# A conditioned transformer block on one core: second MLP product token-major, two head groups' denominators from the exps, prologue reordered, two scheduler constants changed

## The chip, the cores and the metric

The kernel runs on 1 core of one Trainium2 chip. The metric is the time on the device in microseconds (us), from the core's first instruction to its last and a little more; the profile's span is 1 to 3 us shorter than the time. The lower the better.

## The reference

One block: layer norm with conditioning, multi-query attention (32 heads of 32, one shared K and V), and a gated MLP. S = 2048 tokens, D = 1024, F = 3584, everything in bf16.

```python
mod = (silu(c) @ w_mod).reshape(1, 6, 1, -1)
sa, ca, ga, sb, cb, gb = ...                     # six rows of 1024
h = layernorm(x) * (1 + ca) + sa
q = h @ wq      # 32 heads of 32
k = h @ wk      # one head of 32, shared
v = h @ wv      # one head of 32, shared
p = softmax(q k^T * 32**-0.5)
x = x + ga * ((p v) @ wo)
h = layernorm(x) * (1 + cb) + sb
x = x + gb * ((silu(h @ w1) * (h @ w3)) @ w2)
```

## The kernel before

The kernel treats the tokens in 4 blocks of 512 queries. For each block there is `attention` (8 head groups of 4 heads) and then `post` (output projection, layer norm, first products with w1 and w3, second product with w2). The `post` of one block is interleaved with the `attention` of the next. What runs when is decided by a list scheduler inside the kernel: every operation is a node with an assumed duration; the scheduler walks through an imagined time and gives each engine, again and again, the best node that could start now. The result is a fixed instruction order per engine. Semaphores keep it correct; the assumed times set only the order and the PSUM banks (PSUM is where TensorE writes its results; the kernel uses it as 8 banks of 512 columns).

```python
def act_t(n):                         # assumed ScalarE time for n columns
    return n / 1200.0 + 0.115
...
# in schedule(): the pick on TensorE ("pe"); S = scores, V = value matmuls, D = denominators
    def key(c):
        s, n = c
        if n.cls == "S":
            r = 0
        elif n.cls is not None:
            r = 1 if att or t - n.est > 1.0 else 4
        else:
            r = 3                     # MLP and projection matmuls: the fill
        return (r, n.prio, n.seq)
pick = min((c for c in cands if c[0] <= t + (slack if c[1].prio <= 1 else 0.001)), key=key)
...
st = max(dma_free, s + 1.2)           # assumed DMA time
dma_free = st + n.nbytes / 230e3
```

Attention, per head group: 16 steps. A step makes scores for one tile of 128 keys and four heads (4 matmuls into PSUM), two exps of 128 x 1024 on ScalarE into one of `NU = 10` buffers, and after 8 steps a batch of 32 value matmuls that reads those 8 buffers. The softmax denominators come from VectorE, which adds four exp tiles into a partial sum (`TR`, 3 adds each), and 16 matmuls with ones over the four partial sums.

```python
NU = 10; VB = 8; NTR = 5
for s in range(ns):                   # 16 steps
    u = i % NU
    ...                               # scores -> SP, two exps SP -> U[u]
    if len(pend) == vb:               # every 8 steps: 32 value matmuls
        ...
    # partial sums on VectorE
    if w == 1:   TR[tr] = U[first_u] + U[u]
    elif w > 1:  TR[tr] = TR[tr] + U[u]
# denominators: ones x TR, 4 partial sums x 4 heads
```

Second product, with the output transposed (128 rows of D by 512 tokens), so it has to be turned back by transposes:

```python
for dt in range(NC):
    o2t[dt] = sum over fc of  W2S[fc].T @ HHT[fc, 0:512]     # 28 matmuls of 512 columns
    O2B = o2t[dt] * gate_column                              # VectorE
    transpose 4 x (128x128), then X += ...                   # TensorE, VectorE
```

Start: the loads stand in one queue in program order.

```python
xload(0, 4); <8 loads of modulation columns>; <wk, wv, wq part 0>; xload(4, 4); <wq rest>; <wo>
# then, with the work on the tiles: xload(8, 4), xload(12, 4)
```

The softmax here doesn't subtract the row's maximum and nothing guards it: scores larger than these inputs give would overflow.

Of the kernel before, what the change touches and what calls it, by code (L numbers as in the profile page):

```python
# [8 lines left out]
P = 128  # L9
# [4 lines left out]
class Node:  # L14
    __slots__ = ("eng", "fn", "dur", "lat", "deps", "prio", "seq", "mode", "acq", "touch",
                 "start", "vis", "pos", "ndeps", "users", "need_inc", "cnt", "dsem", "dval", "nbytes", "est", "cls",
                 "sbanks")
# [8 lines left out]
class Dag:  # L26
# [12 lines left out]
    def add(self, eng, fn, reads=(), writes=(), dur=0.1, lat=0.1, prio=5, mode=None, cls=None,  # L39
            acq=None, groups=(), seq=None, dkey=None, nbytes=0, sbanks=()):  # L40
# [41 lines left out]
        for d in n.deps:  # L82
            d.users.append(n)
        n.dsem = n.dval = None
# [9 lines left out]
    def schedule(self, banks):  # L94
# [8 lines left out]
        for n in self.nodes:  # L103
            n.ndeps = len(n.deps)
            n.est = 0.0
            if n.ndeps == 0:
                ready[n.eng].append(n)
# [28 lines left out]
        while left:  # L136
# [85 lines left out]
            if n.dsem is not None:  # L222
                st = max(dma_free, s + 1.2)
                dma_free = st + n.nbytes / 230e3
                n.vis = dma_free + 0.8
            else:
                n.vis = s + d + n.lat
            for u in n.users:
                u.ndeps -= 1
                if not (e == "pe" and u.eng == "pe"):  # L230
                    u.est = max(u.est, n.vis + SEM_LAT)
                if u.ndeps == 0:
                    ready[u.eng].append(u)
# [73 lines left out]
def act_t(n):  # L307
    return n / 1200.0 + 0.115
# [9 lines left out]
def build(nc, x_in, wq_in, wk_in, wv_in, wo_in, w1_in, w3_in, w2_in, c_in, wmod_in, out, S, D, F):  # L318
# [12 lines left out]
    R = 4  # L331
    NTR = 5
# [12 lines left out]
    WREG = sb("WREG", [P, 4 * 2048 + 2 * NF * P], BF16)  # L345
# [14 lines left out]
    NM = sb("NM", [P, NT], F32)  # L360
# [7 lines left out]
    O2B = HREG[:, o + 1024:o + 2048].rearrange("p (a s) -> p a s", a=2)  # L368
# [6 lines left out]
    U = UREG[:, 0:NU * 2048].rearrange("p (u g s) -> p u g s", u=NU, g=4)  # L375
    TR = UREG[:, NU * 2048:].rearrange("p (u g s) -> p u g s", u=NTR, g=4)
    WM01 = UREG[:, 0:NC * 2048].rearrange("p (c s) -> p c s", c=NC)
    assert (NU + NTR) * 2048 >= NC * 2048
    W1S = WREG[:, 0:2 * 2048].rearrange("p (a c f) -> p a c f", a=2, c=NC)
    W3S = WREG[:, 2 * 2048:4 * 2048].rearrange("p (a c f) -> p a c f", a=2, c=NC)  # L380
    W2S = WREG[:, 4 * 2048:].rearrange("p (a c f) -> p a c f", a=2, c=NF)
    WQ = WREG[:, 4 * 2048 - 2048:4 * 2048 - 2048 + NC * D].rearrange("p (c f) -> p c f", c=NC)
    WMS = WREG[:, 0:6144].rearrange("p (a c f) -> p a c f", a=3, c=4)
    GAB = WREG[:, 4 * 2048 - 2048 + NC * D:4 * 2048 - 2048 + NC * D + 1024]

    SP = nc.alloc_psum_tensor("SP", [P, 3, 2, 512], F32)
    PB = [nc.alloc_psum_tensor("PB%d" % i, [P, 512], F32)[:] for i in range(2)]
    PB += [SP[:, b, h, :] for b in range(3) for h in range(2)]
# [13 lines left out]
    def dma(fn, key, reads=(), writes=(), nbytes=0, prio=5, seq=None):  # L402
        return G.add("sp", fn, reads=reads, writes=writes, dur=0.06, dkey=key, nbytes=nbytes, prio=prio, seq=seq)
# [3 lines left out]
    def xload(t0, n):  # L407
        for t in range(t0, t0 + n):
            dma(lambda e, t=t: e.dma_start(X[:, t % NXS, :], x2[t * P:(t + 1) * P, :]),
                ("x", t % NXS), writes=[("X", t % NXS)], nbytes=P * D * 2)  # L410

    xload(0, 4)
    for k in range(NC):
# [7 lines left out]
    xload(4, 4)  # L421
    dma(lambda e: e.dma_start(WQ[:, :, P:D], wq_in[:, P:D].rearrange("(c p) f -> p c f", p=P)), "wq1",
        writes=[("WQ", 1)], nbytes=7 * P * D * 2)
    dma(lambda e: e.dma_start(WO[:], wo_in.rearrange("(c p) f -> p c f", p=P)), "wo", writes=["WO"], nbytes=D * D * 2)
# [41 lines left out]
    def ln_scale(t0, n):  # L466
        ks = [("MV", t0 + i) for i in range(n)]
        rk = [("RS", t0 + i) for i in range(n)]
        G.add("pool", lambda e: e.tensor_scalar(RS[:, t0:t0 + n], MV[:, t0:t0 + n, 1], EPS, None, ALU.add),
              reads=ks, writes=rk, dur=0.3)  # L470
        G.add("pool", lambda e: e.tensor_tensor(RS[:, t0:t0 + n], RS[:, t0:t0 + n], NHALF[:, 0:n], ALU.pow),
              reads=rk + ["NHALF"], writes=rk, dur=0.4)
        G.add("pool", lambda e: e.tensor_tensor(NM[:, t0:t0 + n], RS[:, t0:t0 + n], MV[:, t0:t0 + n, 0], ALU.mult),
              reads=rk + ks, writes=[("NM", t0 + i) for i in range(n)], dur=0.3)

    def ln_norm(t, q):
        s = t % NXS
        G.add("dve", lambda e: e.tensor_scalar(XN[:, q, :], X[:, s, :], RS[:, t:t + 1], NM[:, t:t + 1],
                                               ALU.mult, ALU.subtract),
              reads=[("X", s), ("RS", t), ("NM", t)], writes=[("XN", q)], dur=0.5, prio=2)  # L480

    def ln_transpose(nt, q0, dst, dkeys, fs, fm, engs, prio=5):
# [3 lines left out]
        for cb in range(NC // ncb):  # L486
            g = grp()
            for i in range(nt):
                def tr(e, i=i, g=g, cb=cb):
                    for h in range(ncb):  # L490
                        c = cb * ncb + h
                        r = e.transpose(PBH[g.bank][:, h * w + i * P:h * w + (i + 1) * P],
                                        XN[:, q0 + i, c * P:(c + 1) * P], IDENT[:])
                    return r
                G.add("pe", tr, reads=[("XN", q0 + i), "IDENT"], dur=ncb * 0.065, lat=0.2,
                      acq=g if i == 0 else None, groups=[(g, "w")], mode="F", prio=prio)
            for h in range(ncb):
                c = cb * ncb + h
                en = engs[cb % len(engs)]
                if en == "act":  # L500
# [4 lines left out]
                        dur=act_t(w) + 0.19, prio=2)  # L505
# [49 lines left out]
    for tb in range(NTB):  # L555
        for i in range(4):
            ln_stats(tb * 4 + i)
        ln_scale(tb * 4, 4)
        for i in range(4):
            ln_norm(tb * 4 + i, i)  # L560
        if tb + 2 < NTB:
            xload(tb * 4 + 8, 4)
        ln_transpose(4, 0, lambda c, tb=tb: HT[:, c, tb * 512:(tb + 1) * 512],
                     lambda c, tb=tb: [("HT", c, tb)], 0, 1, ("act", "dve") if tb == 0 else ("dve",))
        kv(tb)
        if tb == 0:
            qproj(0, 0)
    for f in range(1, NC):
# [5 lines left out]
    nwm = 0  # L574
    GAK = [("GAB",)]
    for h in range(2):
        g = grp()
        for kb in range(2):
            sl = nwm % 3
            nwm += 1  # L580
            dma(lambda e, kb=kb, h=h, sl=sl: e.dma_start(
                WMS[:, sl], wmod_in[kb * 512:(kb + 1) * 512, 2 * D + h * 512:2 * D + (h + 1) * 512]
                .rearrange("(c p) f -> p c f", p=P)), ("wms", sl), writes=wms(sl), nbytes=P * 2048 * 2)
            def mm(e, kb=kb, sl=sl, g=g):
                for k in range(4):
                    i = e.matmul(PB[g.bank], SCB[kb * 4 + k], WMS[:, sl, k, :],
                                 start=(kb == 0 and k == 0), stop=(kb == 1 and k == 3))
                return i
            G.add("pe", mm, reads=SCBK + wms(sl), dur=4 * MM, lat=0.2, acq=g if kb == 0 else None,
                  groups=[(g, "w")], mode="F")  # L590
        G.add("dve", lambda e, g=g, h=h: e.tensor_copy(GAB[:, h * 512:(h + 1) * 512], PB[g.bank]),
              writes=[("GAB", h)], groups=[(g, "r")], dur=dve_t(512), prio=4)
    for f in range(NC):
        G.add("dve", lambda e, f=f: e.tensor_tensor(WO[:, f, :], WO[:, f, :], GAB, ALU.mult),
              reads=["WO", ("GAB", 0), ("GAB", 1)], writes=[("WOG", f)], dur=dve_t(1024, 2), prio=6)
    for m in range(3):
        g = grp()
        for h in range(2):
            for kb in range(2):
                sl = nwm % 3  # L600
                nwm += 1
# [14 lines left out]
        a, b2 = ((1.0, 0.0), (1.0, 1.0), (0.5, 0.0))[m]  # L616
        G.add("dve", lambda e, g=g, m=m, a=a, b2=b2: e.tensor_scalar(
            MODC[:, 3 + m, :], PB[g.bank][:, 0:8], a, b2, ALU.mult, ALU.add),
            writes=[("MODC", 3 + m)], groups=[(g, "r")], dur=0.15, prio=4)
    for tb in range(1, NTB):  # L620
# [7 lines left out]
    def attention(q0, qn):  # L628
        npk = 512 // qn
        ns = NT // npk  # L630
        per_t = ns // (R // npk)
        vb = VB // npk
        for f in range(NC):
            pend = []
            trs = []
            for s in range(ns):
# [3 lines left out]
                bufs = [(2 * i) % 3, (2 * i + 1) % 3]  # L640
                kts = [s * npk + j for j in range(npk)]

                def smm(e, f=f, kts=kts, bufs=bufs):
                    for j, kt in enumerate(kts):
                        for gg in range(4):
                            r = e.matmul(SP[:, bufs[gg // 2], gg % 2, j * qn:(j + 1) * qn],  # L646
                                         KT[32 * gg:32 * gg + 32, kt * P:(kt + 1) * P],
                                         QT[32 * gg:32 * gg + 32, f, q0:q0 + qn], start=True, stop=True,
                                         tile_position=(32 * gg, 0))
                    return r  # L650
                G.add("pe", smm, reads=sorted({("KT", kt // 4) for kt in kts}) + qkeys(f, q0, qn),
                      writes=[("SP", b) for b in bufs], dur=npk * qn / 2400 + 0.027 * npk, lat=0.2, prio=0, cls="S",
                      mode="S", sbanks=[2 + 2 * b + h for b in bufs for h in range(2)])
                uk = [("UR", u)]
                for h in range(2):
                    G.add("act", lambda e, u=u, h=h, b=bufs[h]: e.activation(  # L656
                        U[:, u, 2 * h:2 * h + 2, 0:npk * qn], SP[:, b, :, 0:npk * qn], ACT.Exp, scale=SCALE),
                        reads=[("SP", bufs[h])], writes=[("U", u, h)] + (uk if h == 0 else []), dur=act_t(2 * npk * qn),
                        prio=0, sbanks=[2 + 2 * bufs[h] + a for a in range(2)])
                ur = [("U", u, 0), ("U", u, 1)] + uk  # L660
                pend.append((u, kts))
                if len(pend) == vb:
                    g = grp()
                    last = len(pend) - 1
                    for w0 in range(0, len(pend), 2):
                        def pv(e, part=tuple(pend[w0:w0 + 2]), f=f, g=g, w0=w0, last=last):
# [231 lines left out]
```

## Time and profile before

| before | |
|---|---|
| time, median of the first 3 runs (lowest to highest) | 1310.71 us (1310.08 to 1313.36) |
| span, mean granted clock of TensorE | 1308.6 us, 0.935 |
| first exp, exp no. 25, exp no. 257, end of last exp | 29.2, 83.7, 320.6, 1107.7 us |
| exps | 1024, started 0.905 us apart (median of all start-to-start times) |

The first view is the page: busy time of each engine, then the busy tenths in 40 slices of 32.7 us. "PEclk" is the granted clock in tenths.

```profile
span 1308.6 us, 21172 instructions
...
PE 1138.8 (87%) x8561; PEld 439.4 (34%) x8689; DVE 958.9 (73%) x1206; ACT 1015.3 (78%) x1142; POOL 17.1 (1%) x35
...
PE   5387896455779999999899999999999999999998
...
ACT  1368988999999999999979999998999998011100
PEclk8688996666889999999999999999999999999999
```

ScalarE is full up to slice 34 and then almost empty; TensorE is full from about slice 12 to the end. So there is an attention stretch, in which exps and matmuls both nearly fill their engine, and a tail that is matmuls alone. I cut the span at exp no. 25 (the first that needs late K tiles), at exp no. 257 (the first of block 1) and at the end of the last exp. The windows view of before gives, for each stretch, its length and then busy time and instruction count by engine:

```profile
core 0: us, PE busy (x) PEld busy (x) DVE busy (x) ACT busy (x) POOL busy (x), PEclk, DMA share, GB/s
0.00:83.70 83.70, 42.40 (x506) 24.94 (x511) 58.05 (x116) 26.80 (x30) 8.87 (x23) 0.76 0.58 197
83.70:320.60 236.90, 166.88 (x1467) 54.83 (x1480) 168.47 (x186) 216.42 (x232) 0.00 (x0) 0.78 0.17 46
320.60:1107.70 787.10, 735.70 (x5611) 269.45 (x5703) 655.67 (x782) 755.37 (x853) 6.77 (x9) 0.99 0.32 84
1107.70:1308.60 200.90, 193.85 (x980) 90.15 (x997) 76.71 (x122) 16.74 (x29) 1.47 (x3) 0.99 0.53 127
```

Blocks 1 to 3 (third row) have ScalarE busy for 755 of 787 us and TensorE for 736. The tail (fourth row) has TensorE busy for 194 of 201.

Where ScalarE idles at the start: its timeline (start, length, engine, line, operation, count, and in brackets the idle time before it and what ended it), and below it two lines of the DMA queue.

```profile
39.96 9.27 ACT L656 ACTIVATE UREG<-SP 128x1024 bf16<-128x1024 f32 x10 [0.82 <-PE SP L646]
73.86 7.44 ACT L656 ACTIVATE UREG<-SP 128x1024 bf16<-128x1024 f32 x8 [24.64 <-PE SP L646]
83.73 20.84 ACT L656 ACTIVATE UREG<-SP 128x1024 bf16<-128x1024 f32 x22 [2.43 <-PE SP L646]
```

```profile
21.33 10.25 SPq L581 DMA_DIRECT2D WREG<-in_w_mod_dram  x3
31.70 39.35 SPq L409 DMA_DIRECT2D X<-in_A_x_dram  x16
```

The x tiles stand behind the modulation and weight loads, and exp no. 17 waits 24.64 us for scores whose K comes from those tiles.

```profile
437.35 6.94 ACT L656 ACTIVATE UREG<-SP 128x1024 bf16<-128x1024 f32 x7
```

Seven fill matmuls stand in one interval between scores, the 32 value matmuls in the next, 2.2 us each. The exp pair that covers an interval takes 1.8 us; ScalarE shows no wait here.

### The profile page before, as it was taken

The page shows a single profiled execution, that of the slowest core. Times are in us where ns is not written, and L with a number is a line of the kernel's source. Part 1 is how long each engine was busy: PE and PEld are TensorE (multiplying, and loading weights), DVE is VectorE, ACT ScalarE, POOL GpSimd, SP SyncE. Part 2 cuts the span into 40 slices and gives each one's busy share as a digit, 9 for nine tenths or more (in the row PEclk, how much of TensorE's full clock was granted, in tenths as well). Part 3 has the DMA queues.
Part 4 walks back from the last instruction along what each step waited for, and adds up shares of the span by engine and source line. Part 5 has one row for each costly group of instructions (what it writes and reads, how often), then busy time and mean ns, then how long its engine had stood idle before and what let it go on. Part 6 is the DMA issues. An engine that isn't in the chain of part 4 may idle for free.

```text
span 1308.6 us, 21172 instructions
## 1 busy us (share of the span) xinstructions
PE 1138.8 (87%) x8561; PEld 439.4 (34%) x8689; DVE 958.9 (73%) x1206; ACT 1015.3 (78%) x1142; POOL 17.1 (1%) x35
## 2 busy tenths in 40 slices
PE   5387896455779999999899999999999999999998
PEld 3133331111223333333333333333333333444443
DVE  5768786666798888778978887789888887643421
ACT  1368988999999999999979999998999998011100
POOL 1000000000000000000000000000000000000000
PEclk8688996666889999999999999999999999999999
DMA  9415104000003333342423333441533334375545
GB/s 313 151 41 178 33 1 110 12 1 1 1 1 97 98 97 97 94 85 57 120 78 94 95 94 94 93 77 29 157 97 98 97 97 85 77 175 147 160 83 118
DMA packets 253504, 118.93 MB, mean 91 GB/s; under 512 B 121312, under 2 KB 245216, under 8 KB 253408
## 3 DMA queue, kind: packets, MB, share of 16 engines
q1 hardware_dynamic: 253408, 117.59, 33.9%
q8 instruction: 68, 1.11, 0.4%
q14 instruction: 28, 0.23, 0.1%
HBM read 113.38 MB, written 4.19 MB: 90 GB/s over the span
## 4 chain that ended last, share of the span: by engine, by line
PE 58%; ACT 25%; DVE 9%; issue 6%; DMA 1%; POOL 1%; SPq 0%; DVEq 0%; ACTq 0%
ACT UREG L656 24%; PE PB L765 13%; PE PB L794 10%; PE PB L670 8%; PE SP L646 7%; PE SP L765 6%; PE SP L794 4%; PE PB L546 3%; PE PB L738 2%; ACT HREG L774 2%; DVE UREG L697 2%; DVE ST L461 1%; DVE UREG L702 1%; PE PB L712 1%; PE SP L738 1%
## 5 line engine op out<-in xcount | busy, mean ns | idle before, releaser
L656 ACT ACTIVATE UREG<-SP 128x1024 bf16<-128x1024 f32 x1024 | 968.5, 1067 | 85.5 <-PE SP L646 65.9
L765 PE MATMUL PB<-QT,WREG 128*128 128x512 bf16 x1397 | 343.3, 381 | 9.1 <-issue 6.4
L702 DVE TENSOR_TENSOR UREG<-UREG 128x2048 bf16<-128x2048 bf16 x256 | 310.5, 1213 | 38.4 <-ACT UREG L656 35.9
L646 PE MATMUL SP<-QT,KT 32*128 32x512 bf16 x2048 | 215.4, 411 | 100.0 <-ACT UREG L656 93.9
L697 DVE TENSOR_TENSOR UREG<-UREG 128x2048 bf16<-128x2048 bf16 x128 | 155.8, 1217 | 70.0 <-ACT UREG L656 69.9
L765 PEld LDWEIGHTS PB<-QT,WREG 128*128 128x128 bf16 x1456 | 125.7, 98 | 176.2 <-issue 52.3
L646 PEld LDWEIGHTS SP<-QT,KT 32*128 32x128 bf16 x2048 | 52.0, 92 | 313.4 <-ACT UREG L656 287.0
L794 PE MATMUL PB<-HREG,WREG 128*128 128x512 bf16 x612 | 153.3, 380 | 4.0 <-issue 2.5
L670 PE MATMUL PB<-UREG,V 128*32 128x512 bf16 x2016 | 142.9, 419 | 6.2 <-ACT UREG L656 5.8
L721 DVE RECIPROCAL DSB<-DSB 128x128 f32<-128x128 f32 x128 | 115.5, 928 | 0.1
L774 ACT ACTIVATE HREG<-SP 128x512 bf16<-128x512 f32 x28 | 16.7, 597 | 126.8 <-PE SP L765 123.9
L781 DVE TENSOR_TENSOR HREG<-HREG,PB 128x512 bf16<-128x512 bf16 x98 | 66.3, 676 | 19.6 <-PE PB L765 18.6
L794 PEld LDWEIGHTS PB<-HREG,WREG 128*128 128x128 bf16 x644 | 55.3, 98 | 73.5 <-issue 22.9
L765 PE MATMUL SP<-QT,WREG 128*128 128x512 bf16 x330 | 74.5, 379 | 0.3
L670 PEld LDWEIGHTS PB<-UREG,V 128*32 128x32 bf16 x2016 | 48.0, 101 | 78.9 <-issue 32.4
L776 DVE SCALAR_TENSOR_TENSOR HREG<-HREG,PB 128x512 bf16<-128x512 bf16 x84 | 57.5, 685 | 13.0 <-ACT HREG L774 9.9
L546 PE MATMUL PB<-HREG,WREG 128*128 128x512 bf16 x243 | 62.2, 389 | 1.7 <-DVE QT L549 0.8
L774 ACT ACTIVATE HREG<-PB 128x512 bf16<-128x512 f32 x84 | 56.5, 672 | 6.9 <-PE PB L765 6.8
L794 PE MATMUL SP<-HREG,WREG 128*128 128x512 bf16 x245 | 56.0, 379 | 0.4
L738 PE MATMUL PB<-WO,QT 128*128 128x512 bf16 x193 | 51.0, 389 | 2.9 <-DVE X L741 1.2
L776 DVE SCALAR_TENSOR_TENSOR HREG<-HREG,SP 128x512 bf16<-128x512 bf16 x28 | 19.3, 688 | 43.4 <-ACT HREG L774 43.4
L765 PEld LDWEIGHTS SP<-QT,WREG 128*128 128x128 bf16 x336 | 32.8, 98 | 39.4
(81 smaller groups left out, 547.9 us busy)
## 6 DMA issues: line engine op xcount, KB each, us to landing
WREG<-in_B_w_dram SPq DMA_DIRECT2D x112, 512.0 KB, 3.9
WREG<-in_B_w_dram SPq DMA_DIRECT2D x32, 896.0 KB, 5.9
X<-in_A_x_dram SPq DMA_DIRECT2D x32, 256.0 KB, 3.6
WREG<-in_w_mod_dram SPq DMA_DIRECT2D x16, 512.0 KB, 5.0
UREG<-in_w_mod_dram SPq DMA_DIRECT2D x8, 512.0 KB, 7.9
out_dram<-X SPq DMA_DIRECT2D x16, 256.0 KB, 2.6
WO<-in_A_wo_dram SPq DMA_DIRECT2D x1, 2048.0 KB, 14.6
WREG<-in_A_wq_dram SPq DMA_DIRECT2D x1, 1792.0 KB, 9.6
```

What stands on the lines that cost most here:

```text
L546: g = mm_group(NC, lambda e, b, c: e.matmul(b, WQ[:, c, f * P:(f + 1) * P], HT[:, c, sl], start=c == 0, stop=c == NC - 1), lambda c: [("WQ ...
L646: r = e.matmul(SP[:, bufs[gg // 2], gg % 2, j * qn:(j + 1) * qn], KT[32 * gg:32 * gg + 32, kt * P:(kt + 1) * P], QT[32 * gg:32 * gg + 32, ...
L656: G.add("act", lambda e, u=u, h=h, b=bufs[h]: e.activation(U[:, u, 2 * h:2 * h + 2, 0:npk * qn], SP[:, b, :, 0:npk * qn], ACT.Exp, scale=S ...
L670: r = e.matmul(PB[g.bank][32 * gg:32 * gg + 32, 0:qn], V[:, kt, :], U[:, pu, gg, j * qn:(j + 1) * qn], start=w0 + n == 0 and j == 0, stop= ...
L697: G.add("dve", lambda e, tr=tr, u=u, fu=first_u: e.tensor_tensor(TR[:, tr, :, 0:npk * qn], U[:, fu, :, 0:npk * qn], U[:, u, :, 0:npk * qn] ...
L702: G.add("dve", lambda e, tr=tr, u=u: e.tensor_tensor(TR[:, tr, :, 0:npk * qn], TR[:, tr, :, 0:npk * qn], U[:, u, :, 0:npk * qn], ALU.add), ...
L721: G.add("dve", lambda e, h=h: e.reciprocal(DSB[:, h * 128:(h + 1) * 128], DSB[:, h * 128:(h + 1) * 128]), reads=["DSB"], writes=[("DSBr", ...
L738: g = mm_group(NC, lambda e, b, f, t=t, h=h: e.matmul(b, QT[:, f, t * P:(t + 1) * P], WO[:, f, h * 512:(h + 1) * 512], start=f == 0, stop= ...
L765: return e.matmul(b[:, o:o + qn], w13[w][:, sl, c, sub * P:(sub + 1) * P], QT[:, c, q0:q0 + qn], start=c == 0, stop=c == NC - 1)
L774: G.add("act", lambda e, g=g1: e.activation(TS[:, 0:qn], PB[g.bank][:, 0:qn], ACT.Tanh, scale=0.5), writes=["TS"] + alias("TS"), groups=[( ...
L776: G.add("dve", lambda e, g=g1: e.scalar_tensor_tensor(TT[:, 0:qn], TS[:, 0:qn], 1.0, PB[g.bank][:, 0:qn], ALU.add, ALU.mult), reads=["TS"] ...
L794: return e.matmul(b[:, j * qn:(j + 1) * qn], W2S[:, (d0 + j) % 2, fc, :], HHT[:, fc, 0:qn], start=fc == 0, stop=fc == NF - 1)
```

## The change

The change has several parts in one diff (cut to the core):

- **Second product token-major**: the activations are the stationary operand, `w2` streams, the output is token by D and needs no transposes. Matmuls are twice as many at half the columns. The gate becomes a row that is multiplied in at evacuation. The w2 slots share their space with those of w1 and w3, so each load is 1.75 MB.
- **Direct denominators** for two of eight head groups in blocks 1 to 3 (`NDIR = 2`): 32 more ones matmuls per batch of 8 steps instead of VectorE's adds.
- **LN2 per tile**, and the reciprocals of the last head group with higher priority.
- **Prologue**: 8 x tiles come first, then the modulation columns; the rest of wq, and wo, after all x loads. With it, x tiles 4 to 7 are normalised into other space, and half of the second tiles' evictions from PSUM go to ScalarE.
- **Two constants** of the scheduler: assumed ScalarE time (`act_t`, called the exp constant below) and assumed DMA rate.

```diff
 def act_t(n):
-    return n / 1200.0 + 0.115
+    return n / 1200.0 + 0.057
@@ schedule
-                dma_free = st + n.nbytes / 230e3
+                dma_free = st + n.nbytes / 300e3
@@ prologue
-    xload(0, 4)
+    xload(0, 8)
     <modulation columns, wk, wv, wq part 0>
-    xload(4, 4)
-    dma(... WQ[:, :, P:D] ...)
-    dma(... WO ...)
+    ... after the last x load: dma(... WQ[:, :, P:D], after=xl); dma(... WO, after=xl)
@@ attention
+            direct = f < ndirect
-                    <32 value matmuls>
+                    for kind, dst in (("V", ASB), ("D", DSB))[0:2 if direct else 1]:
+                        g = batch(pend, kind, qn)      # 32 matmuls each
+                if direct:
+                    continue                           # no adds on VectorE
@@ post
-        ln_scale(t0, nt)
-        for i in range(nt):
-            ln_norm(t0 + i, i)
+            ln_scale(t, 1)                             # inside the loop over tiles
+            ln_norm(t, i)
...
-                return e.matmul(b[:, j * qn:(j + 1) * qn], W2S[:, (d0 + j) % 2, fc, :], HHT[:, fc, 0:qn], ...)
-    <gate column at evacuation, 4 transposes per 128 rows, add to X>
+                    return e.matmul(b[:, j * 256:(j + 1) * 256], HHT[:, fc, (i0 + j) * P:(i0 + j + 1) * P],
+                                    W2S[:, r, fc, :], ...)
+    <times gate row GBB at evacuation, add to X>
@@ build
+    FIVE = 9          # never reached: there are 4 blocks
+    NDIR = 2
```

## The prediction

> **What bounds the kernel now.** The timeline by engine shows three stretches. (1) Start, 0 to 84 us: ScalarE's first exp is at 29.2 us; after 16 it idles 24.6 us (waits: exp on the scores matmul), because K and V of tokens 1024 and up are missing. Their layer-norm statistics begin at 50.5 us: their x loads stand behind WQ, WO and three modulation loads in the DMA queue. (2) Middle, 84 to 1107.7 us: ScalarE-bound, an exp every 0.94 us, about 49 us of idle: 6 beside the modulation loads, some 20 in block 0 (granted clock about 0.64), about 24 in blocks 1 to 3. The PE is nearly full there (windows: 48 of 50 us); what does not fit spills. (3) Tail, 1107.7 to 1308.6 us: no exps; PE without pause: the rest of block 2's second product (about 28 us), output projection, first products 96.7 us, second product about 50 us. VectorE (73% busy) bounds nothing long.
>
> **What the change does** (counts from both kernels' instruction order, durations from the trace).
> - Prologue: eight x tiles come before the modulation columns, the next eight before WQ and WO. First exp at 33 to 34 us (1 MB more ahead of it). VectorE's work up to the last K eviction ends at about 64 us, so exp 25 comes at about 65, not 83.7 us: **minus 19**.
> - Direct denominators, two of eight head groups in blocks 1 to 3: VectorE loses 72 adds of 1.2 us, about 87 us, off the critical path. The PE gains 6 x 48 row-tiled matmuls at 0.054 us (16 take about 0.86): **plus 15.6 us**. The PE being full, the second product spills: 875 half-size matmuls after the last scores matmul, against 363 whole ones before.
> - Token-major product: twice the matmuls at half the columns. Whole ones run 0.2157 us apart (33 in 7.12). The Trainium skill, "TensorE: Matmul & The Clock Gate", section "Back-to-back issue gap", gives columns/2.4 + 2.5 ns, which this trace confirms at 512 columns; my estimate for 256 is 0.109 us: neutral. 128 transposes go (7 us, 3 in the tail); the end chain shortens by 1.5.
> - Shared weight space: in the tail the first 1.8 MB second-product load cannot start until the last four first-product groups (6.9 us); I estimate 8.5 us, so 1.5 to 2 us of stall.
> - LN2 per tile, high-priority reciprocals: cleaner transitions; but denominator batches of 32 stand beside 7 fill matmuls between two scores matmuls, 1.6 to 1.8 us over the exp pair. Gaps in blocks 1 to 3: 24 before, 24 to 30 after.
>
> **Sum.** Last exp at 1107.7 - 19 + 2 = 1091 us. Tail: second product 78 + 3 becomes 95.5, plus stall, minus shorter end: 200.9 + 14 = 215. Span 1306, less 2 for cleaner transitions: **1304 us**, range **1286 to 1319**; chances **0.13** faster by over 2%, **0.84** within, **0.03** slower.
>
> **What would show each step right.** First exp at 33 to 34 us; 24 exps done by about 65; last exp at 1080 to 1098; 213 to 219 us from it to the end, PE back to back; VectorE about 85 us less busy; exps unchanged in count and length; second product 0.109 us apart in the tail; one wait of 1 to 3 us on the weights DMA at its start.
>
> **What would make it wrong.** If 256-column matmuls cost much more than half, the tail grows by up to 20 us. If the middle gaps nearly vanish, 1285. If x lands late behind 4 MB of modulation, the 19 shrink. If transitions starve exps more, 1315.

## More of the kernel before

The exps of before started 0.905 us apart (median of all start-to-start times). ScalarE's waits in blocks 1 to 3 of before (in total, how many, the longest):

```profile
ACT UREG L656 <- PE PB L670: 11.6, 6, 3.7
ACT UREG L656 <- PE SP L646: 10.6, 25, 2.2
ACT HREG L774 <- PE PB L765: 6.8, 4, 3.2
```

That is 29.0 us. "UREG <- PE PB" is an exp that waits until the value matmuls have read the buffer it will overwrite; "UREG <- PE SP" is an exp that waits for its scores; "HREG <- PE PB" is the gate's activation (a tanh, half of the silu) that waits for its first product.

One place in detail, which will be compared later: steps 9 and 10 of head group 3 in block 1 (counted from 0), on TensorE and on ScalarE. L646 are scores, L765 first-product matmuls (the fill), L670 value matmuls.

```profile
436.39 0.40 PE L646 MATMUL SP<-QT,KT 32*128 32x512 bf16 x4
436.72 1.68 PE L765 MATMUL PB<-QT,WREG 128*128 128x512 bf16 x7
438.61 0.39 PE L646 MATMUL SP<-QT,KT 32*128 32x512 bf16 x4 [0.20 <-ACT UREG L656]
438.93 1.91 PE L670 MATMUL PB<-UREG,V 128*32 128x512 bf16 x32
440.77 0.40 PE L646 MATMUL SP<-QT,KT 32*128 32x512 bf16 x4
```

## The result and the profile after

| | before | after |
|---|---|---|
| time, median (lowest to highest), 4 runs each | 1311.88 us (1310.08 to 1313.36) | 1312.81 us (1312.48 to 1313.78) |
| span, mean granted clock | 1308.6 us, 0.935 | 1311.7 us, 0.956 |
| to exp no. 25 | 83.7 | 65.0 |
| rest of block 0 (exp 25 to 257) | 236.9 | 234.0 |
| blocks 1 to 3 (exp 257 to end of last) | 787.1 | 798.5 |
| tail | 200.9 | 214.2 |

The ratio of after to before is 1.0009, 95% interval 0.9992 to 1.0026: the same time. Ratios here and below are the mean time of one kernel's runs over that of the other's of the same rounds, so not quite the ratio of the medians quoted. The forecast of 0.5% less did not come: 21.6 us won in the first two stretches were given back in the last two, 11.4 and 13.3.

The page of after:

```profile
span 1311.7 us, 23162 instructions
...
PE 1174.4 (90%) x9697; PEld 520.3 (40%) x9697; DVE 880.2 (67%) x1137; ACT 1009.1 (77%) x1146; POOL 20.8 (2%) x51
```

The windows of after, cut at the same four events (columns as above):

```profile
0.00:65.00 65.00, 37.59 (x510) 22.60 (x511) 54.31 (x111) 29.40 (x35) 8.09 (x19) 0.95 0.75 253
65.00:299.00 234.00, 168.83 (x1432) 53.71 (x1430) 170.54 (x189) 214.51 (x233) 0.00 (x0) 0.81 0.13 39
299.00:1097.50 798.50, 759.35 (x6311) 307.66 (x6312) 576.04 (x710) 748.48 (x853) 9.55 (x24) 0.99 0.29 81
1097.50:1311.70 214.20, 208.63 (x1448) 136.30 (x1445) 79.31 (x128) 16.74 (x29) 3.17 (x8) 1.00 0.48 133
```

ScalarE's timeline at the start of after, and TensorE's first scores:

```profile
38.26 1.94 ACT L715 ACTIVATE UREG<-SP 128x1024 bf16<-128x1024 f32 x2 [4.46 <-PE SP L704]
44.05 20.27 ACT L715 ACTIVATE UREG<-SP 128x1024 bf16<-128x1024 f32 x22 [3.85 <-PE SP L704]
64.97 25.79 ACT L715 ACTIVATE UREG<-SP 128x1024 bf16<-128x1024 f32 x28 [0.65 <-PE SP L704]
```

```profile
37.54 0.61 PE L704 MATMUL SP<-QT,KT 32*128 32x512 bf16 x4 [5.21 <-DVE HREG L515]
```

The 24.64 us wait is gone and exp no. 25 starts at 64.97 us. The first exp comes later than foreseen, because the first scores matmul waits 5.21 us for VectorE's evictions of the second x tiles.

ScalarE's waits in blocks 1 to 3 of after (L704 are scores, L809 first-product matmuls; L659 is the line of all batches of 32, the value matmuls and, in the direct head groups, also the matmuls with ones; "waits on the batches" below means both):

```profile
ACT UREG L715 <- PE PB L659: 44.1, 24, 3.3
ACT UREG L715 <- PE SP L704: 3.9, 3, 1.6
ACT HREG L818 <- PE PB L809: 1.9, 2, 1.1
```

That is 49.9 us, against 29.0 before. The stretch grew by less, 11.4 us: ScalarE's idle time grew by 18.3 us, but it was busy 6.9 us less with the same 853 instructions (third rows of the windows), whose records overlap more. The same steps of the same head group in after, TensorE and then ScalarE:

```profile
419.47 0.39 PE L704 MATMUL SP<-QT,KT 32*128 32x512 bf16 x4
419.80 1.69 PE L809 MATMUL PB<-QT,WREG 128*128 128x512 bf16 x7
422.24 1.91 PE L659 MATMUL PB<-UREG,V 128*32 128x512 bf16 x32 [0.76 <-DVE HREG L820]
424.09 0.40 PE L704 MATMUL SP<-QT,KT 32*128 32x512 bf16 x4
```

```profile
422.91 4.69 ACT L715 ACTIVATE UREG<-SP 128x1024 bf16<-128x1024 f32 x5 [2.09 <-PE PB L659]
```

What before had in two intervals, 7 fill matmuls and 32 value matmuls, after has in one, with a 0.76 us wait for a PSUM bank in between: 4.6 us from scores to scores, and ScalarE loses 2.09 us. Ten of the 24 waits are of this kind, 2.08 or 2.09 us long, all at step 10 of an ordinary head group.

Twelve of the others are ended by a batch of ones instead, the direct denominators, which has been put between the same scores as value matmuls or fill. The first of them, TensorE and then ScalarE:

```profile
322.76 1.91 PE L659 MATMUL PB<-UREG,ONES 128*32 128x512 bf16 x32
```

```profile
323.43 14.77 ACT L715 ACTIVATE UREG<-SP 128x1024 bf16<-128x1024 f32 x16 [1.65 <-PE PB L659]
```

Sorted by what stood on TensorE when the wait ended, the 44.1 us are 24.1 on value matmuls (12 waits) and 20.0 on ones (12 waits).

Second product in the tail, before (L794) and after (L838):

```profile
1259.73 6.21 PE L794 MATMUL SP<-HREG,WREG 128*128 128x512 bf16 x27
```

```profile
1258.23 6.29 PE L838 MATMUL SP<-WREG,HREG 128*128 128x256 bf16 x56 [1.18 <-DMA WREG<-in_B_w_dram]
```

The 56 half-size matmuls start 6.12 us before those of the next group (1264.35): 0.109 us each. The stall for the shared weight space is the 1.18 us in brackets.

### The profile page after: what moved, and what is told of

Read it like the earlier page. It is cut to its first block, busy times and chain, and to the rows that moved or that the text cites. A ratio compares the mean times of both kernels' runs of the same rounds, so it can differ in the third digit from the quotient of the medians. Undisturbed runs are those within 1.5% of the kernel's fastest.

```text
span 1311.7 us, 23162 instructions
## 1 busy us (share of the span) xinstructions
PE 1174.4 (90%) x9697; PEld 520.3 (40%) x9697; DVE 880.2 (67%) x1137; ACT 1009.1 (77%) x1146; POOL 20.8 (2%) x51
## 4 chain that ended last, share of the span: by engine, by line
PE 48%; ACT 37%; DVE 6%; issue 6%; DMA 2%; SPq 1%; ACTq 0%; DVEq 0%
ACT UREG L715 35%; PE PB L809 12%; PE PB L659 6%; PE SP L704 6%; PE SP L838 6%; PE PB L838 5%; PE SP L809 5%; PE PB L786 3%; PE PB L554 2%; ACT HREG L818 2%; DVE UREG L744 2%; PE PB L760 2%; DVE UREG L749 1%; DMA UREG<-in_w_mod_dram 1%; PE SP L786 1%
## 5 line engine op out<-in xcount | busy, mean ns | idle before, releaser
L809 PE MATMUL PB<-QT,WREG 128*128 128x512 bf16 x1456 | 355.9, 380 | 0.4
L704 PE MATMUL SP<-QT,KT 32*128 32x512 bf16 x2048 | 212.9, 406 | 84.3 <-ACT UREG L715 71.4
L749 DVE TENSOR_TENSOR UREG<-UREG 128x2048 bf16<-128x2048 bf16 x208 | 253.2, 1217 | 39.0 <-ACT UREG L715 37.3
L744 DVE TENSOR_TENSOR UREG<-UREG 128x2048 bf16<-128x2048 bf16 x104 | 126.1, 1212 | 101.4 <-ACT UREG L715 101.4
L809 PEld LDWEIGHTS PB<-QT,WREG 128*128 128x128 bf16 x1456 | 123.4, 98 | 177.7 <-issue 60.1
L704 PEld LDWEIGHTS SP<-QT,KT 32*128 32x128 bf16 x2048 | 51.9, 91 | 296.6 <-ACT UREG L715 286.5
L659 PE MATMUL PB<-UREG,V 128*32 128x512 bf16 x2048 | 143.7, 411 | 11.0 <-DVE HREG L820 7.6
L838 PE MATMUL PB<-WREG,HREG 128*128 128x256 bf16 x1120 | 141.2, 273 | 1.2 <-DVE HREG L843 1.2
L838 PEld LDWEIGHTS PB<-WREG,HREG 128*128 128x128 bf16 x1120 | 102.7, 98 | 38.9 <-issue 24.4
L659 PEld LDWEIGHTS PB<-UREG,V 128*32 128x32 bf16 x2048 | 47.1, 100 | 83.2 <-issue 31.7
L838 PE MATMUL SP<-WREG,HREG 128*128 128x256 bf16 x672 | 75.0, 273 | 1.2 <-DMA WREG<-in_B_w_dram 1.2
L809 PE MATMUL SP<-QT,WREG 128*128 128x512 bf16 x336 | 75.0, 379 | 0.0
L838 PEld LDWEIGHTS SP<-WREG,HREG 128*128 128x128 bf16 x672 | 65.6, 98 | 10.1 <-DMA WREG<-in_B_w_dram 1.7
L818 ACT ACTIVATE HREG<-PB 128x512 bf16<-128x512 f32 x84 | 64.9, 773 | 1.9 <-PE PB L809 1.9
L554 PE MATMUL PB<-HREG,WREG 128*128 128x512 bf16 x256 | 63.6, 381 | 0.7 <-DVE QT L557 0.5
L786 PE MATMUL PB<-WO,QT 128*128 128x512 bf16 x208 | 54.6, 390 | 0.3 <-DVE DSB L727 0.3
```

Of the source, the lines that this page charges most:

```text
L554: g = mm_group(NC, lambda e, b, c: e.matmul(b, WQ[:, c, f * P:(f + 1) * P], HT[:, c, sl], start=c == 0, stop=c == NC - 1), lambda c: [("WQ ...
L659: r = e.matmul(PB[g.bank][32 * gg:32 * gg + 32, 0:qn], V[:, kt, :] if kind == "V" else ONES[:], U[:, pu, (gg * npk + j) * qn:(gg * npk + j ...
L704: r = e.matmul(SP[:, b, o:o + w], KT[32 * gg:32 * gg + 32, kts[j] * P:(kts[j] + 1) * P], QT[32 * gg:32 * gg + 32, f, q0 + qo:q0 + qo + w], ...
L744: G.add("dve", lambda e, tr=tr, u=u, fu=first_u: e.tensor_tensor(TR[:, tr, 0:4 * W], U[:, fu, 0:4 * W], U[:, u, 0:4 * W], ALU.add), reads= ...
L749: G.add("dve", lambda e, tr=tr, u=u: e.tensor_tensor(TR[:, tr, 0:4 * W], TR[:, tr, 0:4 * W], U[:, u, 0:4 * W], ALU.add), reads=[("TR", tr) ...
L786: g = mm_group(NC, lambda e, b, f, t=t, h=h: e.matmul(b, QT[:, f, t * P:(t + 1) * P], WO[:, f, h * 512:(h + 1) * 512], start=f == 0, stop= ...
```

## The experiments

Sixteen kernels ran, in four rounds, each timed against before on the same chip (medians of before 1312.19, 1312.52, 1311.24 and 1310.83 us; three chips in all, so kernels of different rounds are best compared by their ratios). All gave correct results. Stretches are taken from each run's own trace at the same four events. "Plain counts" below are counts of instructions in the kernel's TensorE order.

### Round 1: the direct denominators, or the scheduler's exp constant?

My first reading was that the direct denominators filled TensorE and so caused both the longer tail and the waits. The rival was that the two scheduler constants had changed the order. The assumed exp (1024 columns) had gone from 0.968 to 0.910 us. The same line sets the assumed tanh of the gate (512 columns, from 0.542 to 0.484 us), so every edit of it below moves both.

**e1_no_direct**: after without direct denominators.

```diff
-    NDIR = 2
+    NDIR = 0
```

> The changed kernel without direct denominators (all head groups use the VectorE adds again). Theory D (the direct denominators put 15.6 us of work on a full PE and so spill it into the tail): 12 to 16 us faster than the changed kernel, about 1298, tail down by as much. Theory M (the instruction order got worse because the scheduler's assumed exp time was shortened by 58 ns): only 6 to 10 us faster, about 1304; the order has 819 half-size second-product matmuls after the last scores matmul against 875, so the tail falls by 6 us only, and the waits of the exps in blocks 1 to 3 stay near 40 us.

Measured 1310.43 us (1307.06 to 1311.85), ratio 0.9981 (0.9961 to 1.0001). The tail went from 214.2 to 209.1, blocks 1 to 3 from 798.5 to 800.5. ScalarE's waits on the batches add up to the same, 44.2 us (20 waits), but they are not the same waits: with no direct denominators left, value matmuls end all of them. The direct denominators therefore cost almost nothing in sum. That is an exchange and no proof that they made no waits: in after, 20.0 us are ended by them.

**e2_exp_model**: after with the old exp constant.

```diff
-    return n / 1200.0 + 0.057
+    return n / 1200.0 + 0.115
```

> The changed kernel with one constant of its scheduler set back (assumed exp time 0.968 us in place of 0.910[...]): no instruction is added or removed, only the order moves. Theory M: exps' waits in blocks 1 to 3 fall from 44 to about 26 us, 745 half matmuls after the last scores matmul in place of 875 (tail down 14 us): 25 to 32 us faster than the changed kernel, about 1284. Theory D: within 4 us of the changed kernel.

Measured 1288.40 us (1287.53 to 1289.64), ratio 0.9822 (0.9808 to 0.9837): 24.4 us faster than after, although no operation and no exp buffer differs, only the order and with it the PSUM banks. Windows of blocks 1 to 3 and tail, and ScalarE's waits in blocks 1 to 3:

```profile
297.30:1085.80 788.50, 750.85 (x6367) 323.53 (x6440) 574.57 (x715) 755.30 (x853) 9.95 (x24) 0.98 0.31 85
1085.80:1286.20 200.40, 193.99 (x1307) 123.67 (x1317) 76.86 (x124) 16.72 (x28) 3.28 (x8) 1.00 0.47 130
```

```profile
ACT UREG L715 <- PE PB L659: 23.6, 11, 4.3
ACT UREG L715 <- PE SP L704: 5.9, 12, 1.6
```

Blocks 1 to 3 fell by 10.0 us and the tail by 13.8, which is nearly everything that after had given back. Of the 23.6 us of waits on the batches only 0.4 are still on value matmuls (24.1 in after); 23.2 are on ones (20.0 in after). The constant took away the first kind and left the second. Plain counts agree: after the last scores matmul, 875 half-size second-product matmuls are left in after, 745 here; 130 of them at 0.109 us are 14.2 us.

**e3_both**: both edits.

> The changed kernel with both edits: no direct denominators, old exp constant. Theory M: about as e2 (order has 784 half matmuls in the tail, 39 more than e2, so plus 4 us there; fewer denominator matmuls between exps, minus a few): 1278 to 1290. Theory D: about 1298, as e1.

Measured 1287.49 us (1284.05 to 1288.87), ratio 0.9811 (0.9792 to 0.9829), within 1 us of e2. With the old constant, too, the direct denominators don't matter to the total, but they do move time: without them the waits on the batches fall from 23.6 to 8.9 us and blocks 1 to 3 from 788.5 to 781.0, while the tail grows from 200.4 to 207.0.

**e4_before_short_exp**: the new constant alone, on before.

```diff
-    return n / 1200.0 + 0.115
+    return n / 1200.0 + 0.057
```

> The kernel before with only the assumed exp time shortened as in the change. Theory M: the exps' waits in blocks 1 to 3 rise from 26 us by 10 or more, 8 stretches of 18 first-product matmuls and a value batch of 32 stand between two scores matmuls (about 4 us each): 8 to 25 us slower than before. Theory D: within 3 us of before.

Measured 1340.43 us (1339.5 to 1342.22), ratio 1.022 (1.0205 to 1.0235): the one line costs before 28 us. Its blocks 1 to 3 grew from 787.1 to 820.4 us, its tail stayed (199.4). ScalarE's waits there:

```profile
ACT UREG L656 <- PE PB L670: 40.5, 17, 6.5
ACT HREG L774 <- PE PB L765: 21.3, 8, 3.2
```

So the constant is the cause in both kernels, and where it is paid (waits alone, or waits and tail) depends on the rest. No run separates its effect through the exps from that through the tanh.

### Round 2: what the other parts are worth

**e5_before_prologue**: before with only the reordered prologue (loads, x tiles 4 to 7 normalised into other space, half of the second tiles' evictions on ScalarE, assumed DMA rate 300), old exp constant.

```diff
-    xload(0, 4)
+    xload(0, 8)
...
-    xload(4, 4)
-    dma(... WQ rest ...); dma(... WO ...)
+    ... both after the last x load
-                dma_free = st + n.nbytes / 230e3
+                dma_free = st + n.nbytes / 300e3
-                     ..., 0, 1, ("act", "dve") if tb == 0 else ("dve",))
+                     ..., 0, 1, ("act", "dve") if tb < 2 else ("dve",))
```

> The kernel before with only the reordered prologue (x tiles first, WQ and WO later, two more LN tiles buffered, half of the second tile's evictions on ScalarE); the order after the prologue is the same as before, count for count. If the prologue's gain of 21.6 us at the 257th exp, seen in the changed kernel, is carried to the end: about 1290. If it is given back later (an engine that is ahead waits elsewhere): 1300 to 1310.

Measured 1288.79 us (1287.28 to 1290.42), ratio 0.9814 (0.9795 to 0.9833). Exp no. 25 at 64.5 us, block 0's rest 232.9, blocks 1 to 3 789.7, tail 200.9. The prologue alone brings 1.9%, and what it wins at the start arrives at the end.

**e6_rest_without_prologue**: e3 with the old prologue, so token-major product, gate row and LN2 per tile alone (with the small edits that came with them).

```diff
-    xload(0, 8)
+    xload(0, 4)
...                                   (and the other prologue edits of e5 undone)
```

> The changed kernel with the old prologue, without direct denominators and with the old exp constant, so the token-major product, the gate at eviction and LN2 per tile remain. If these are neutral, as predicted: 1305 to 1313, e3 plus 21 us. If the token-major product costs (weights reload badly hidden, waits on its 1.8 MB loads): above 1318. If it gains: below 1302.

Measured 1305.44 us (1304.72 to 1309.39), ratio 0.995 (0.9931 to 0.9969). Exp no. 25 at 84.5, blocks 1 to 3 781.0, tail 207.2. These parts are worth 0.3 to 0.7% on the old prologue; on the new one e3 and e5 differ by nothing that the intervals show.

**e7_more_exp_buffers**: after with one more exp buffer and one partial sum less.

```diff
-    NU = 10
-    NTR = 5
+    NU = 11
+    NTR = 4
```

> The changed kernel with 11 buffers for exps in place of 10 (and 4 for partial sums in place of 5). The traces put the exps' waits in blocks 1 to 3 on the value matmuls, that is on a buffer of exps being free. If the ring of 10 with batches of 8 is what turns a late value batch into a ScalarE wait, the waits on value matmuls fall from 42 to under 20 us. The order, though, leaves 267 first-product matmuls (58 us) more in the tail: total 1325 to 1350, slower. If buffers are not the reason, the waits stay near 40 us and the total is above 1360.

Measured 1328.65 us, ratio 1.0121 (1.0106 to 1.0136). The waits on the batches in blocks 1 to 3 fell from 44.1 to 7.4 us and the stretch to 751.7, but the tail rose to 278.4: in the new order, 267 more first-product matmuls come after the last scores. Fewer waits were no gain, since ScalarE ran ahead and left TensorE's work for the end. The order moved with the buffers, so this run did not say whether the buffers themselves were the limit; e13 does.

**e8_longer_exp_model**: e1 with a longer constant still.

```diff
-    return n / 1200.0 + 0.057
+    return n / 1200.0 + 0.150
```

> As e3 (no direct denominators), but with the assumed exp time lengthened further, to 1.003 us[...]: the order packs more matmuls between exps and leaves 609 half matmuls in the tail in place of 784, so the tail falls by 19 us; the exps wait more in the middle. If the PE's packing is what the total hangs on: 1272 to 1285, below e3. If packing and waiting cancel: 1285 to 1295.

Measured 1301.08 us, ratio 0.9911 (0.9896 to 0.9926). Against e3, which differs in the constant alone, the tail fell from 207.0 to 192.8 and blocks 1 to 3 rose from 781.0 to 809 us; exps start 0.920 us apart in the median there, 0.905 in e3. A longer assumed exp puts more fill into the attention stretch; beyond some point it delays the exps by more than the tail gains.

### Round 3: is the accurate constant best?

**e9_true_exp_model**: e1 with + 0.083, which I then took for the true value.

> As e3 (no direct denominators), but with the assumed exp time [...]0.936 us, between e1 (0.910, 1310 us) and e3 (0.968, 1287 us). If it is the mismatch with the chip that costs, this is the best of the three: 1285 or less. If the constant matters only by how many matmuls the order packs between exps, then the order decides: it leaves 13 us more of PE work after the last scores matmul than e3, so about 1295 to 1303.

Measured 1290.41 us, ratio 0.9837 (0.9822 to 0.9852), between what the two theories expected: blocks 1 to 3 773.4, tail 218.2. The premise was wrong, and has to be corrected here. The 0.936 us in that text, and the 0.94 us in the prediction, are too high: busy time per exp (968.5 us for 1024 in before) also holds the overhang at the end of every run of exps, and waits too short to show between overlapping records. Start to start, the median is 0.905 us in before and 0.904 in after, and e2 and e9 have the same. The constant that the change put in (0.910 us for an exp) is the accurate one; the old one (0.968) is 7% too long, and is the faster. For the tanh it is the same: 0.478 us from its start to the next exp's (median where nothing waits, in before and in after), 0.484 assumed.

**e10_buffers_and_model, e11_buffers_model_130, e12_buffers_model_150**: `NU = 11`, `NTR = 4`, `NDIR = 0`, with constants 0.115, 0.130 and 0.150.

> e3 with 11 buffers of exps and 4 of partial sums. The tail order holds 3 us less PE work than e3, and the waits on value matmuls should fall from 9 us to below 5: 1278 to 1286. If the ring was not limiting at this constant: 1284 to 1290, as e3.

> As e10 with the assumed exp time at 0.983 us: 10 us less PE work in the tail than e10, one stretch of 7.6 us of PE work between two scores matmuls and somewhat more waits in the middle: 1275 to 1288.

> As e10 with 1.003 us: tail 13 us shorter than e10's, waits in the middle up by 10 to 15: 1278 to 1292. e8 showed at 10 buffers that packing beyond this costs more in waits than the tail returns; if that holds at 11 buffers too, above e11.

Measured 1294.72, 1290.88 and 1297.31 us, ratios 0.987 (0.9855 to 0.9884), 0.9834 (0.9818 to 0.9851) and 0.9889 (0.9874 to 0.9904). All three came out slower than the ranges I gave (e12 met its second expectation, above e11). Their tails are 202.8, 193.9 and 192.1 us. An 11th buffer with one partial sum less is no step beyond e3, at any constant tried.

### Round 4: same order, one more buffer

The waits of after are named as exp on the batches, that is, as a full ring of 10 exp buffers. Whether the ring is the cause can be seen only if the order stays. For e13 the scheduler ran as in after with 10 buffers, the orders of all engines and the PSUM banks were recorded, and the kernel was emitted from that record with 11. Space for the 11th came from small tiles that share space after their last use. e14 is the control: the same with 10.

```diff
+    def replay(self, record):          # order and banks from the record, no scheduling
...
-    NU = 10
+    NU = 10 for the record, then 11 (e13) or 10 (e14) for the kernel that is emitted
```

> The changed kernel's own instruction order on all engines, with 11 exp buffers in place of 10 (the space comes from letting small prologue tiles share others). If the ring is what holds the exps: the waits on value matmuls in blocks 1 to 3 fall from 44 to under 15 us, and these blocks from 799 to 775 to 787 us (ScalarE's own work there is about 773); total 1288 to 1302. If the PE is late in any case: the waits move to the scores matmul and the total stays within 6 us of the changed kernel, 1306 to 1314.

> As e13 with 10 buffers: the shared small tiles alone. Both theories: within 3 us of the changed kernel, 1310 to 1316.

Measured: e13 1307.23 us, ratio 0.997 (0.9956 to 0.9985); e14 1312.89 us, ratio 1.0015 (1.0 to 1.003), as after. ScalarE's waits in blocks 1 to 3 of e13, and the same place on TensorE:

```profile
ACT UREG L729 <- PE SP L718: 42.5, 27, 3.1
```

```profile
417.33 1.68 PE L823 MATMUL PB<-QT,WREG 128*128 128x512 bf16 x7
419.77 1.91 PE L673 MATMUL PB<-UREG,V 128*32 128x512 bf16 x32 [0.76 <-DVE HREG L834]
421.62 0.40 PE L718 MATMUL SP<-QT,KT 32*128 32x512 bf16 x4
```

No exp waits for a batch any more, and 42.5 us of waits stand there all the same, now on scores. TensorE passes through the same 7 + 32 matmuls, with the same 0.76 us wait for a bank, and is late with the next scores. The ring gave the wait its name; the order gave it its length. What the ring itself was worth is the difference to the control, some 6 us.

**e15_e3_order_11_buffers and e16_e9_order_11_buffers**: the same with the orders of e3 and of e9.

> The order of e3 with 11 buffers. e3 waits 9 us on value matmuls in blocks 1 to 3. Ring: 1278 to 1284. PE late: 1285 to 1289, as e3.

> The order of e9[...] with 11 buffers. e9 waits 18 us on value matmuls there and has the longest tail of the good orders, 218 us. Ring: 1272 to 1282. PE late: 1286 to 1291, as e9.

Measured 1287.17 us, ratio 0.9821 (0.9805 to 0.9838), and 1288.65 us, ratio 0.9833 (0.9818 to 0.9848). Neither is distinguishable from e3 or e9.

## Why the prediction was right or wrong

The sum, by spans: measured −18.7 (start), −2.9 (rest of block 0), +11.4 (blocks 1 to 3), +13.3 (tail): +3.1 us. Predicted were −19, then +2 up to the last exp and −2 for cleaner transitions, and +14: −5 us.

**Right: the prologue.** Exp no. 25 at 64.97 us against "about 65". e5 shows that the gain is worth its full size in the total. The first exp missed its step (38.3 us against 33 to 34): the first scores matmul waited for evictions that share its PSUM banks. It cost nothing, because the K of later tiles set exp no. 25: its scores still waited 0.73 us for VectorE's eviction of that K.

**Right in size, wrong in its main cause: the tail.** 214.2 us against 215, the last exp at 1097.5 (range given 1080 to 1098), half-size matmuls 0.109 us apart as estimated, one stall of 1.18 us. But the prediction put the longer tail down to the "plus 15.6 us" of direct denominators. e1 takes them away and the tail falls by 5.1 us only, the total by 2.4. e2 leaves them in, and the tail falls by 13.8. Most of the spill came from the exp constant, which the prediction did not mention though it stood in the diff. The size agreed because I counted the spill from the finished instruction order, which contains the constant's effect, whatever I believed its reason to be.

**Right: VectorE and the neutral parts.** VectorE's busy time fell by 78.7 us (958.9 to 880.2, "about 85"), and no run shows that this was worth anything: the waits for VectorE shown above (5.21 us at the first scores, 0.76 us in ten places) are for evictions, not for the adds that went. 1024 exps as before; one exp lasts longer in the records (median 1.042 to 1.144 us), but they start 0.905 and 0.904 us apart, so that costs nothing. Token-major product, gate row and LN2 per tile, predicted as about neutral, are between nothing and 0.7% (e6, e3 against e5).

**Wrong: "Gaps in blocks 1 to 3: 24 before, 24 to 30 after"**, and with it "less 2 for cleaner transitions". This is the step that failed. By the waits view the gaps are 29.0 before and 49.9 after, and the stretch grew by 11.4 us instead of shrinking. Three things were wrong in it.

1. The intervals between two scores matmuls that run 1.6 to 1.8 us over an exp pair were seen, but I counted them as mostly absorbed by the buffers. They were not: in the first with ones, scores to scores takes 3.68 us (320.92 to 324.60) for a pair of exps that takes 1.81, which is 1.87 over, and ScalarE loses 1.65 of these. Longer ones were not seen: in the place shown at 419.47, it is 4.62 us (to 424.09), 2.81 over, with the 0.76 us wait for a PSUM bank in it, and ScalarE loses 2.09. Ten places are alike.
2. They were put down to denominator batches alone. Those make half of the waits on the batches in after: 20.0 us, which is by itself more than the 0 to 6 that the prediction allowed. The other 24.1 us, the ten places among them, are on batches of 32 **value** matmuls of ordinary head groups; all waits on batches in before were of that kind, and came to 11.6 us.
3. The cause of the waits on value matmuls is the constant, which the prediction left out. With the same operations and the old constant (e2) they fall from 24.1 to 0.4 us and blocks 1 to 3 to 788.5; with the new constant alone (e4) before goes from 29.0 to 68.6 us of waits (40.5 + 21.3 + 6.8). The waits on ones stay in e2 (23.2 us) and go with the direct denominators (e3), at the price of a longer tail.

Why does an accurate constant make a worse order? One hint, which is a count from the kernel's own schedule and no measurement: adding up the gaps that the scheduler itself plans on ScalarE in blocks 1 to 3 gives 25 us for before, 55 for after, 80 for e4 and 21 for e2. So the waits were in the plan; the chip did not surprise it. (The planned end is no guide: 1294 us for after, 1303 for e2, the wrong way round.) The same count, with the new constant set back for the exps alone or for the tanh alone in after, gives 25 and 30 us in place of 55, so both can matter to the order; neither was run. The scheduler is greedy: it fills TensorE with whatever can start now, and pays for that at the next scores. With shorter exps less TensorE time passes per exp pair, and in the middle of head groups fill and value batch fall into the same interval. An exp that is assumed 7% too long leaves slack in the plan, and on the chip part of that slack is taken back. This fits the series without direct denominators: constants 0.057, 0.083, 0.115 and 0.150 gave 1310.4, 1290.4, 1287.5 and 1301.1 us. That the greedy choice is what goes wrong is argued from this, not shown by a run with another rule.

**Best versions.** e3 and e15 (1287.5 and 1287.2 us), e2 (1288.4) and e5 (1288.8) beat both kernels by 1.8 to 1.9%. The simplest is the old kernel with the new prologue, or the new one with the old constant.

**Open.** The best versions end between 1287 and 1289 us with different splits between waits and tail; what would go lower was not found. Why 11 buffers with 4 partial sums (e10 to e12) are no better than e3 was not separated, since their order moved too. The new DMA constant ran only together with the new prologue, so its own share is not known. Nor is it known how much of the exp constant's effect goes through the assumed tanh.

## What to carry to other kernels

When an instruction order is computed from assumed durations, a changed constant is a change to the whole kernel: undo it alone, first, before looking for costs in the operations that changed beside it. A more accurate constant need not give a better order, so choose it by measured time. A wait's releaser in the profile names what ended it, not what caused it: keep the order fixed, lift that releaser, and see whether the time goes or the wait just takes another name (here 44.1 us on the batches became 42.5 on scores). And a line number can stand for two kinds of work: sort its waits by tile before blaming one of them.

## What the Trainium skill lacked or had wrong

- The Trainium skill, "TensorE: Matmul & The Clock Gate", section "Back-to-back issue gap", calls columns/2.4 + 2.5 ns the gap of an isolated matmul and gives about 131 ns per matmul as sustained at 512 columns. Here a stream in the tail of before, each matmul with its own weights load, ran 0.2157 us apart (33 in 7.12 us): the formula's value, not 131 ns. For 256 columns the page lists no sustained figure; the trace of after has 0.109 us (56 in 6.12 us), which the formula gives too.
- The same page, section "Measured speedup vs the span model", has 3.07x for four row tiles and 2.38x for three column tiles. In after, 32 value matmuls of 512 columns on four column tiles, queued, took 1.85 us from the first's start to the next instruction's (422.24 to 424.09): 0.058 us each, about 3.7 times as fast as 0.2157. Four column tiles are not in its table.
- No page has a figure for how low the mean granted clock gets when TensorE pauses often but briefly. In before, from 225 to 320 us, it was 0.63, with TensorE busy for 47.87 of 95 us and no wait on exps longer than 1.4 us.
- "ScalarE: Activation LUTs", section "What ACT_TABLE_LOAD costs", gives 186 ns + 0.833 ns per element (1039 ns at 1024) and an overlap of about 93 ns between back-to-back instructions, so 946 ns apart. One exp in before lasted 1.042 us (median), which agrees, but they started 0.905 us apart: an overlap of 0.137 us. In after, one lasted 1.144 us, at the same spacing.
- No page says that a static order made from assumed durations moves by as much as the runs show: 58 ns on the assumed exp were worth 24 us (e2 against after) and 28 us (e4 against before).
